# The last block of an attention and two-MLP kernel: six stores on one queue, or three on two

## The chip, the cores and the metric

The kernel runs on 1 core of one Trainium2 chip. The metric is the device time in microseconds of one execution; lower is better. Before the change it is 937.37 us (median of 3 runs, 936.97 to 937.43).

A core has TensorE (PE, matmul; PEld is its weight load), VectorE (DVE), ScalarE (ACT), GpSimd (POOL) and SyncE (SP), which here only issues transfers (DMAs). Transfers are carried by 16 DMA engines.

## The reference

Windowed attention with a bias per head, then two MLPs over 2304 tokens (4 sequences of 576), model width 512, inner width 2048. Scaled input data left out:

```python
def reference(**kwargs):
    ...
    attn_out = _attn_ref(**attn_kwargs)          # softmax(q k^T / 8 - slope*distance, window 128) v
    B, H, S, D = attn_out.shape                  # 4, 8, 576, 64
    x = np.ascontiguousarray(attn_out.transpose(0, 2, 1, 3)).reshape(B * S, H * D)
    x = _moe_ref(x=x, **moe_kwargs)              # g = s*relu(x w_in)^2 + b;  g w_out
    return _moe2_ref(x=x, **moe2_kwargs)         # relu(x w_in)^2 w_out
```

The output `out` has 2304 rows of 512 float32 (2 KB each). Row `b*576 + s` is token `s` of sequence `b`.

## The kernel before

Attention and the first MLP come first; the change does not touch them. Their result stands in device memory in 9 blocks of 256 tokens: two blocks of 256 from each of the 4 sequences, and a ninth, `LAST`, made of the last 64 tokens (`TAIL`) of all four sequences.

The second MLP takes the tokens in three rounds (`n` = 0, 1, 2) of 768, and the inner width in 8 steps (`NP`) each. A round ends with six tiles `t` = 0 to 5 of 128 tokens by 512 columns, summed up in PSUM tiles `po[(n, t)]`. `way_out(n, t)` (line 876) takes such a tile out: a copy from PSUM into a buffer `ob`, by ScalarE for even `t` and by VectorE for odd `t`, and a store from there to `out`. The pair `(n, t)` is half `t % 2` of block `i = (6n + t) // 2`. So tiles 4 and 5 of the last round are the two halves of the ninth block: tile 4 holds the last 64 tokens of sequences 0 and 1, tile 5 those of sequences 2 and 3. Their rows lie in `out` in two groups of 64, 576 rows apart. Before, each group is stored by a transfer of its own (the loop over `a`). Tile 5 of the last round is in addition split by columns in two halves `x` of 256 (`cols`), the first copied by VectorE, the second by ScalarE.

`result(name, staging)` (line 537) hands out the buffers: with staging true the three buffers that go by the tag `st`, else the two that go by `raw`. They are used in turn; who gets one waits until the store out of it, from its last use, has landed.

The order on the engines is that of the program text from line 913 on (`HANDOVER`, then the loop over `k`); the last calls are `behind(23, 0..11)` (line 950), which run the second layer's last matmuls and `way_out(2, 0)` to `way_out(2, 5)` between them. Instructions on one engine run in order; SP's stores stand in one queue in the order of the copies. All instructions carry line 29 (the recorder's), so the trace is read by tile names: `po` is the PSUM tile, `ob` the buffer, `out` the output.

Of the kernel before, what the change touches and what calls it, by code (L numbers as in the profile page):

```python
# [15 lines left out]
P = 128  # L16
# [75 lines left out]
def attention_mlp2_kernel(ctx, tc, first0, first1, qkv0, qkv1, qkvt, w_in1, w_out1, s_in, b_in, w_in2, w_out2, out):  # L92
# [13 lines left out]
    S, D = NT // B, DM // H  # L106
# [5 lines left out]
    BLK = 256  # L112
# [3 lines left out]
    TAIL = S - 2 * BLK  # L116
# [420 lines left out]
    def result(nm, staging=False):  # L537
        if "bp" in pools:
            return pools["bp"].tile([P, DM], F32, tag="st" if staging else "raw", name=nm, bufs=3 if staging else 2)
        return ap.tile([P, DM], F32, tag="pr", name=nm, bufs=NPR)  # L540
# [29 lines left out]
    LAST = len(blocks) - 1  # L570
# [120 lines left out]
    for i, n in ((6, NCC), (8, 2)):  # L691
        for o in range(n):
            x, y = (2 * o, 2 * o + 1) if i == 6 else (o, o + 2)
# [33 lines left out]
    raws, yf, pairs, po = {}, {}, {}, {}  # L727
# [146 lines left out]
                          stop=(k % NP == NP - 1 and j >= 6 and i == 2), skip_group_check=True)  # L874

    def way_out(n, t):
        ob, i, half = result(f"ob{n}{t}", t % 2 > 0), (6 * n + t) // 2, t % 2
        cols = [slice(0, DM)] if n < 2 or t < 5 else [slice(0, BLK), slice(BLK, DM)]
        for x, c in enumerate(cols):
            (act_copy, vector.tensor_copy)[(t + x) % 2](ob[:, c], po[(n, t)][:, c])  # L880
            for a in range(1 if i < LAST else P // TAIL):
                rows = (i // 2) * S + (i % 2) * BLK + half * P if i < LAST else (half * (P // TAIL) + a) * S + 2 * BLK
                size = P if i < LAST else TAIL
                sync.dma_start(out[rows:rows + size, c], ob[a * size:(a + 1) * size, c])

    for k in range(3 * NP):
        for r in range(4):
# [14 lines left out]
    for n in range(3):  # L902
        for q in range(4):
            table[f"Y{n}.{q}"] = lambda n=n, q=q: load_input(n, q)
            for z in range(2):
                table[f"Z{n}.{q}{z}"] = lambda n=n, q=q, z=z: scale_input(n, q, z)
            table[f"T{n}.{q + 1}"] = lambda n=n, i=q + 1: difference(n, i)
        for m in PRODUCTS:
            table[f"V{n}.{m}"] = lambda n=n, m=m: halve_input(n, m)
        for t in range(6):  # L910
            table[f"O{n}.{t}"] = lambda n=n, t=t: way_out(n, t)
# [15 lines left out]
    for k in range(NP, 3 * NP):  # L927
        n, y = divmod(k, NP)
# [66 lines left out]
```

## Time and profile before

| | before |
|---|---|
| median of 3 runs | 937.37 us (936.97 to 937.43) |
| the profiled execution | 937.67 us |
| its span, first to last instruction | 935.9 us |
| TensorE busy | 904.2 us (97%) |
| VectorE, ScalarE busy | 551.7 us (59%), 504.7 us (54%) |
| mean granted TensorE clock | 0.995 of full speed |

The profile is of one execution. Times within it count from the start of its span. The profiled execution's own time has 1.77 us that lie outside the span. Engines are busy with computing instructions; the issue of a transfer is shown on the queue of the engine that issues it (SPq), with the time that the issue takes, and the time to landing is counted from the start of the issue. The share of the DMA engines is the mean of 16. In a strip of 40 digits each digit is the busy share of a slice in tenths (9 is 90% or more).

### The profile page before, as it was taken

How to read it: one execution, taken by the hardware profiler on the slowest of the kernel's cores; microseconds unless marked ns; L12 is line 12 of the kernel's file. 1: busy time of each engine (PE TensorE's matmuls, PEld its weight loads, DVE VectorE, ACT ScalarE, POOL GpSimd, SP SyncE). 2: the span in 40 equal slices, each digit the busy share in tenths (PEclk: the TensorE clock that was granted, in tenths of full speed). 3: DMA queues.
4: the chain of work that ended last, by engine and by line, in shares of the span. 5: the costliest groups of instructions: out<-in, count | busy, mean ns of one | idle time of the engine just before them, and what ended most of it. 6: DMA issues, size and time to landing. Idle time of an engine off the chain costs nothing.

```text
span 935.9 us, 14604 instructions
## 1 busy us (share of the span) xinstructions
PE 904.2 (97%) x5304; PEld 776.0 (83%) x5304; DVE 551.7 (59%) x1345; ACT 504.7 (54%) x1139; POOL 102.3 (11%) x164
## 2 busy tenths in 40 slices
PE   5899999999999999999999999999999999999997
PEld 3789998877787777777898998887889898989896
DVE  7998775455445545545366988787853436443432
ACT  7988776344344444544366877775653335333332
POOL 4343220000000000000022213222000000000000
PEclk9999999999999999999999999999999999999999
DMA  8633523111012101220125655859996666766312
GB/s 314 209 126 118 180 77 106 46 46 40 23 29 90 46 24 45 79 58 23 65 70 205 230 208 191 306 185 354 338 406 209 182 190 180 237 199 194 101 46 68
DMA packets 70216, 136.75 MB, mean 146 GB/s; under 512 B 8576, under 2 KB 36480, under 8 KB 70144
## 3 DMA queue, kind: packets, MB, share of 16 engines
q1 hardware_dynamic: 70144, 135.82, 43.7%
q8 instruction: 42, 0.69, 0.3%
q14 instruction: 30, 0.25, 0.1%
HBM read 103.29 MB, written 32.51 MB: 145 GB/s over the span
## 4 chain that ended last, share of the span: by engine, by line
PE 81%; DVE 7%; ACT 5%; DMA 4%; issue 2%; SPq 0%; POOL 0%; DVEq 0%; ACTq 0%
PE ha L29 20%; PE oa L29 20%; PE po L29 17%; PE px L29 8%; PE py L29 6%; PE s L29 6%; DMA st<-w_in 2%; PE u L29 2%; DVE st L29 1%; DMA rwil<-first 1%; PE s_t L29 1%; DVE tr L29 1%; ACT st L29 1%; DVE m2wih L29 1%; PE u_t L29 1%
## 5 line engine op out<-in xcount | busy, mean ns | idle before, releaser
L29 POOL TENSOR_TENSOR st<-st 128x256 int32<-128x256 int32 x128 | 94.1, 762 | 269.7 <-DVE st L29 254.3
L29 DVE SCALAR_TENSOR_TENSOR r_all<-ha,r_all 128x256 f32<-128x256 f32 (+1 forms) x96 | 52.8, 554 | 99.4 <-ACT r_all L29 99.4
L29 ACT ACTIVATE r_all<-ha 128x256 f32<-128x256 f32 (+1 forms) x96 | 46.5, 488 | 98.8 <-PE ha L29 94.5
L29 ACT ACTIVATE st<-st 128x512 int32<-128x512 uint32 (+3 forms) x100 | 79.9, 817 | 10.6 <-DMA st<-w_in 5.5
L29 PE MATMUL oa<-ga,woh 128*128 128x256 f32 x384 | 72.5, 288 | 0.1
L29 DVE TENSOR_TENSOR tr<-tr 128x384 f32<-128x384 f32 x96 | 55.1, 575 | 22.3 <-ACT tr L29 22.3
L29 ACT ACTIVATE pr<-pr,nd 128x256 f32<-128x256 f32 (+1 forms) x102 | 48.0, 474 | 29.7 <-DVE nd L29 27.5
L29 PEld LDWEIGHTS oa<-ga,woh 128*128 128x128 f32 x384 | 60.1, 191 | 4.6 <-issue 3.5
L29 ACT ACTIVATE tr<-tr 128x384 f32<-128x384 f32 x72 | 37.7, 524 | 40.7 <-DVE tr L29 40.6
L29 PE MATMUL oa<-ga,wol 128*128 128x256 f32 x192 | 54.3, 283 | 0.0
L29 DVE SCALAR_TENSOR_TENSOR st<-st 128x512 int32<-128x512 int32 (+1 forms) x50 | 41.5, 841 | 10.6 <-ACT st L29 10.0
L29 DVE TENSOR_TENSOR tr<-py,tm 128x384 f32<-128x384 f32 x24 | 13.3, 555 | 44.7 <-PE py L29 43.3
L29 DVE TENSOR_TENSOR m2woh<-tr,m2woh 128x384 fp32r<-128x384 f32 x48 | 27.4, 571 | 20.4 <-ACT m2woh L29 18.6
L29 PE MATMUL po<-m2wih,m2woh 128*128 128x512 f32 x144 | 36.6, 395 | 1.3 <-ACT ob L29 0.9
L29 PE MATMUL po<-m2wih,m2wil 128*128 128x512 f32 x144 | 37.7, 392 | 0.0
L29 ACT ACTIVATE m2woh<-tr 128x384 fp32r<-128x384 f32 x48 | 25.2, 525 | 23.2 <-DVE tr L29 22.8
L29 PE MATMUL po<-m2wih,m2wol 128*128 128x512 f32 x144 | 37.6, 392 | 0.0
L29 PE MATMUL ha<-x0h,wih 128*128 128x256 f32 x128 | 37.3, 292 | 0.0
L29 PE MATMUL ha<-x0h,wil 128*128 128x256 f32 x128 | 36.4, 284 | 0.6 <-DVE wil L29 0.6
L29 PEld LDWEIGHTS oa<-ga,wol 128*128 128x128 f32 x192 | 36.7, 191 | 0.0
L29 PE MATMUL ha<-x0l,wih 128*128 128x256 f32 x128 | 36.2, 283 | 0.0
L29 DVE TENSOR_TENSOR tr<-py,r_all 128x384 f32<-128x384 f32 x24 | 13.3, 556 | 38.5 <-ACT r_all L29 38.4
(606 smaller groups left out, 2436.8 us busy)
## 6 DMA issues: line engine op xcount, KB each, us to landing
m2wih<-wd SPq DMA_DIRECT2D x32, 512.0 KB, 4.5
m2woh<-wd SPq DMA_DIRECT2D x22, 512.0 KB, 4.5
st<-w_out SPq DMA_DIRECT2D x20, 512.0 KB, 4.4
st<-w_in SPq DMA_DIRECT2D x8, 1024.0 KB, 6.4
st<-w_in SPq DMA_DIRECT2D x16, 512.0 KB, 4.7
wd<-m2wih SPq DMA_DIRECT2D x16, 512.0 KB, 6.8
m2wil<-wd SPq DMA_DIRECT2D x16, 512.0 KB, 4.6
st<-w_out SPq DMA_DIRECT2D x6, 1024.0 KB, 7.5
```

The costliest lines, as they stand in the source:

```text
L29: ins = op(*args, **kw)
```

## The change

`way_out` asks `result` for a buffer for each half `x` instead of one for each tile, so the second half of the last tile gets one of its own, from the tag that `(t + x) % 2` says (`raw` for tile 5, `x` = 1). The two groups of 64 rows of the last block leave in one transfer, whose place in `out` has the two sequences as its first dimension. The transfer of the last half tile is issued by ScalarE.

```diff
     def way_out(n, t):
-        ob, i, half = result(f"ob{n}{t}", t % 2 > 0), (6 * n + t) // 2, t % 2
+        i, half = (6 * n + t) // 2, t % 2
         cols = [slice(0, DM)] if n < 2 or t < 5 else [slice(0, BLK), slice(BLK, DM)]
         for x, c in enumerate(cols):
-            (act_copy, vector.tensor_copy)[(t + x) % 2](ob[:, c], po[(n, t)][:, c])
-            for a in range(1 if i < LAST else P // TAIL):
-                rows = (i // 2) * S + (i % 2) * BLK + half * P if i < LAST else (half * (P // TAIL) + a) * S + 2 * BLK
-                size = P if i < LAST else TAIL
-                sync.dma_start(out[rows:rows + size, c], ob[a * size:(a + 1) * size, c])
+            ob = result(f"ob{n}{t}{x}", (t + x) % 2 > 0)[:, c]
+            (act_copy, vector.tensor_copy)[(t + x) % 2](ob, po[(n, t)][:, c])
+            if i < LAST:
+                rows = (i // 2) * S + (i % 2) * BLK + half * P
+                sync.dma_start(out[rows:rows + P, c], ob)
+            else:
+                b0 = half * (P // TAIL)
+                (scalar if x else sync).dma_start(out.rearrange("(b s) n -> b s n", s=S)[b0:b0 + P // TAIL, 2 * BLK:, c], ob)
```

The end of SP's queue, before (-) and after (+). The last numbers in a row are the shape on the side of `out`; `DMAHW` are semaphores that landings count up, used in turn, and the others belong to engines.

```order
 L29 DMA out<-ob_8537 128x512 [waits DMAHW0_49,Activation_49]
 L29 DMA out<-ob_8543 128x512 [waits DMAHW1_49,DVE_49]
-L29 DMA out<-ob_8549 64x512 [waits DMAHW2_49,Activation_49]
-L29 DMA out<-ob_8549 64x512 [waits DMAHW3_49]
-L29 DMA out<-ob_8556 64x256 [waits DMAHW4_49,DVE_49]
-L29 DMA out<-ob_8556 64x256 [waits DMAHW5_49]
-L29 DMA out<-ob_8556 64x256 [waits DMAHW6_49,Activation_49]
-L29 DMA out<-ob_8556 64x256 [waits DMAHW7_49]
-L991 UNCONDITIONAL_BRANCH
+L29 DMA out<-ob_8549 2x64x512 [waits DMAHW2_49,Activation_49]
+L29 DMA out<-ob_8555 2x64x256 [waits DMAHW3_49,DVE_49]
```

Tiles 2 and 3 of the last round (8537, 8543) keep their transfers. Tile 4 (8549) goes from two transfers to one, tile 5 (8556) from four to one here, whose shape begins with a 2.

The end of ScalarE's program, before and after: its copies of tiles 2, 4 and of the second half of 5.

```order
 L29 ACTIVATE ob_8537<-po_7799 128x512 [waits DMAHW2_49,PE_49]
 L29 ACTIVATE ob_8549<-po_7819 128x512 [waits DMAHW6_49,PE_49,Activation_49]
-L29 ACTIVATE ob_8556<-po_7823 128x256 [waits DMAHW3_49,DVE_49]
-L991 UNCONDITIONAL_BRANCH
+L29 ACTIVATE ob_8558<-po_7823 128x256 [waits DMAHW0_49,DVE_49,Activation_49]
+L29 DMA out<-ob_8558 2x64x256 [waits DMAHW4_49,Activation_49]
+L994 UNCONDITIONAL_BRANCH
```

The copy of the last half has a buffer of its own (8558) and waits for `DMAHW0`, the semaphore on which the store of tile 2 lands, in place of `DMAHW3`; the transfer out of it stands behind it on ScalarE. On TensorE, VectorE and GpSimd the order of the instructions is the same.

## Rows read from the trace of the kernel before

**Rows 1.** Chain of waits, the last 11 us: start us, us, what.

```profile
924.84 5.00 PE po L29 x22
...
929.87 0.44 DVE ob L29
...
930.32 0.38 ACT ob L29
```

**Rows 2.** The page's first line.

```profile
span 935.9 us, 14604 instructions
```

**Rows 3.** Time line of ScalarE: start us, us, instruction, [idle before it, releaser].

```profile
929.23 0.60 ACT L29 ACTIVATE ob<-po 128x512 f32<-128x512 f32 x1 [0.81 <-PE po L29]
930.32 0.38 ACT L29 ACTIVATE ob<-po 128x256 f32<-128x256 f32 x1 [0.50 <-DVE ob L29]
```

**Rows 4.** Time line of SP's queue, one issue each: start us, us.

```profile
928.60 0.33 SPq L29 DMA_DIRECT2D out<-ob  x1
...
929.86 0.55 SPq L29 DMA_DIRECT2D out<-ob  x1
930.46 0.59 SPq L29 DMA_DIRECT2D out<-ob  x1
...
932.42 0.55 SPq L29 DMA_DIRECT2D out<-ob  x1
933.02 0.59 SPq L29 DMA_DIRECT2D out<-ob  x1
```

**Rows 5.** Single issues (0.74, 927.09, 928.60, 929.86, 933.02 us): KB, us to landing.

```profile
rwih<-first SPq DMA_DIRECT2D x1, 384.0 KB, 3.1
...
out<-ob SPq DMA_DIRECT2D x1, 256.0 KB, 2.0
...
out<-ob SPq DMA_DIRECT2D x1, 256.0 KB, 2.5
...
out<-ob SPq DMA_DIRECT2D x1, 128.0 KB, 2.4
...
out<-ob SPq DMA_DIRECT2D x1, 64.0 KB, 2.0
```

**Rows 6.** DMA view, 926 to 936 us: packets (counts by size add up), and issues.

```profile
DMA packets 1057, 1.58 MB, mean 158 GB/s; under 512 B 160, under 2 KB 416, under 8 KB 1056
...
out<-ob SPq DMA_DIRECT2D x4, 256.0 KB, 2.3
out<-ob SPq DMA_DIRECT2D x2, 128.0 KB, 2.4
out<-ob SPq DMA_DIRECT2D x4, 64.0 KB, 2.0
```

**Rows 7.** DMA view, 929.4 to 930.4 us: packets; queue's packets, MB, share.

```profile
DMA packets 206, 0.38 MB, mean 377 GB/s; under 512 B 25, under 2 KB 25, under 8 KB 205
...
q1 hardware_dynamic: 205, 0.37, 95.9%
```

**Rows 8.** DMA view, 281.2 to 284.8 us, stores of 1 KB rows.

```profile
DMA packets 1025, 0.94 MB, mean 260 GB/s; under 512 B 112, under 2 KB 1025, under 8 KB 1025
...
q1 hardware_dynamic: 1025, 0.94, 74.2%
```

**Rows 9.** DMA view, 931.2 to 932.2 us.

```profile
DMA packets 126, 0.22 MB, mean 221 GB/s; under 512 B 18, under 2 KB 18, under 8 KB 126
...
q1 hardware_dynamic: 126, 0.22, 91.1%
```

**Rows 10.** DMA view, 932.9 to 934.8 us, with its strip of 40 slices.

```profile
DMA  0246895932000003496985300000246895922000
...
DMA packets 240, 0.20 MB, mean 104 GB/s; under 512 B 48, under 2 KB 240, under 8 KB 240
...
q1 hardware_dynamic: 240, 0.20, 40.5%
```

**Rows 11.** DMA view, strip of 933.2 to 933.8 us.

```profile
DMA  5599541506002000000000000000184515699458
```

## The prediction

> **What bounds the kernel now.** I read the chain of waits first. TensorE's last matmuls run to 929.84 us, then VectorE copies one half of the last tile and ScalarE the other, until 930.70 [rows 1]. Yet the span is 935.9 us [rows 2]: 5.2 us in which no engine computes. The time line of SP's queue fills it: ten transfers leave one by one, and from 929.86 us the six of the last block stand 0.6 us apart, the last at 933.02 [rows 4]. The list of transfers says that one lands 2.0 us after its issue [rows 5], so at 935.0. From there to the end of the span are 0.9 us. So the end is the issue of SP, the landing of the last transfer, and 0.9 us. The change moves nothing ahead of TensorE's last matmul; only the two tiles of the last block, 4 and 5 of the last round, matter.
>
> **What the change removes.** Six transfers on SP become two there and one on ScalarE, for the second half of tile 5. SP's last issue thus moves from 933.02 to the place of today's second, 930.46 [rows 4]: 2.56 us of issue gone, if a new transfer takes about 0.55 us as those of 64 rows do (the ones of 128 rows take 0.33; the new one bears 2x64 rows on one side and 128 on the other, so the ends are 0.33 and, unknown, somewhat over 0.59; as the next issue must wait for VectorE's copy until 930.31 anyhow [rows 1], this decides at most 0.3 us).
>
> **What it adds on ScalarE.** In the order, ScalarE's last copy waited for VectorE's (the two wrote one tile). Its half now has a buffer of its own, but the wait for VectorE stays (I take it that it is for the PSUM tile that both read), and one more comes: the new buffer is one of the two that `result` hands out under the tag raw, and it held tile 2 of this round. So the copy waits until the store of tile 2 is home: issued 928.60 [rows 4], landing 2.5 us later [rows 5], 931.1 us. ScalarE therefore starts its copy at about 931.2 and not at 930.32 [rows 3], takes 0.38 us [rows 3], and issues at about 931.7. Nothing is queued behind it but that issue. The wait alone eats 0.9 us of the gain. With the data spread as today this would land 2.0 to 2.4 us later (64 and 128 KB, [rows 5]), at 933.7 to 934.1, 0.9 to 1.3 us before today's 935.0.
>
> **How the data is spread.** Here I expect the decision. The DMA view of the last 10 us counts 1057 packets, of which 160 are under 512 B, 256 more under 2 KB and 640 of 2 KB [rows 6]. The 640 and 256 are just the rows of the ten transfers (4 x 128 + 2 x 64 of 2 KB, 4 x 64 of 1 KB), so a row is a packet; the 160 are 16 for each transfer, one closing packet from each of 16 engines. So a transfer of 128 rows and one of 64 are both dealt out in 16 equal shares of whole rows. The issue time agrees that SP works on the count of rows and not on bytes: 64 rows of 2 KB and 64 rows of 1 KB cost the same 0.55 to 0.59 us, 128 rows of 2 KB cost 0.33 [rows 4]. Every transfer here had 128 or 64 as the first count on both its sides. The new three have 128 in the buffer but 2 in `out`, since the halves of the block lie a whole sequence apart (the order prints 2x64x512 and 2x64x256). Equal shares along the first count on both sides can then only be two, one sequence each, unless the hardware regroups 2x64 as 128, and the two halves of `out` cannot be written as one step. No row shows a transfer with a first count of 2. The ends are 16 engines and 2; rows of that kind lie nearer to 16, but none has a count that 16 does not divide, so I go by what all have in common, shares along the first count, and take 2.
>
> The Trainium skill, "DMA: Bandwidth & Descriptors", section "Why a DMA increments its semaphore by 16 and not by 1", says it as a rule: the largest number of engines up to 16 that divides the slowest dimension of both access patterns, the lowest-numbered ones being used. It speaks against this change: by it 128 and 2 give 2 engines, the same two for all three transfers; the 16 closing packets of each transfer [rows 6] agree with it for 128 and 64. By the rule the sum is the one that follows; with 16 engines it would be the first rival's.
>
> The price then, on two engines. A packet of 2 KB takes 85 ns when the buffers' 128 rows are stored: 95.9% of 16 engines in 1.0 us are 15.3 us, over 205 - 25 = 180 packets [rows 7]. One of 1 KB takes 47 ns: 74.2% of 16 x 3.6 us are 42.7 us, over 1025 - 112 = 913 [rows 8]. Each engine gets 64 rows of tile 4 (64 x 85 ns = 5.4 us) and 64 + 64 half rows of tile 5 (128 x 47 ns = 6.0 us), 11.4 us in all. ScalarE's queue adds an issuer; I take it that it adds no engine, so its half shares the two and is hidden nowhere. The first packet flows 1.2 us after an issue: that of 932.42 begins at 933.62 (slot 28 of 40 in the strip of [rows 11]), so from 929.86 the data begins at 931.1. Until about then the 16 engines have the older tiles. From 931.1 + 11.4 = 942.5, with 0.3 us from the last packet (934.7, the end of the strip in [rows 10]) to the landing (935.0), and 0.9 us to the end: span 943.7 against 935.9, +7.8 us. The profiled execution took 937.67 us, 1.77 outside its span; the median of the runs is 937.37, 0.30 less. So 937.4 + 7.8 = 945.2 us, 0.8% slower.
>
> Ends of this. Upwards: the last tiles' own packets take longer, 135 ns for 2 KB (91.1% of 16 us over 108, [rows 9]) and 64 ns for 1 KB (40.5% of 30.4 us over 192, [rows 10]), in the transfers of 64 rows; I take the quicker prices because those are of transfers with 128 rows in the buffer, as the new ones are, but at these it is 8.6 + 8.2 = 16.8 us, 950.6. Downwards: 85 and 47 ns leave 38 ns per KB and 9 fixed; if two queues on one engine hide the fixed part, 256 x 38 ns = 9.7 us, 943.5. If ScalarE's half were put on two other engines, 5.4 + 3.0 = 8.4 us, 942.2.
>
> **Rivals.** (1) Not slower: the hardware regroups and keeps 16 engines. Then the last landing is ScalarE's at 933.7 to 934.1, the span ends at 934.6 to 935.0, and the time is 936.1 to 936.5 us, about 936.3: 0.1% faster, which no measurement of this kernel tells from no change (about 0.2%, 1.9 us, is what it can tell). For it: every transfer that the trace shows runs on 16. Against: all of those have one count on both sides. Chance 0.16.
> (2) Faster by over 1.9 us: the last landing would have to come by 933.1. ScalarE's half alone can't, at 931.1 + 0.1 + 0.38 + 0.1 + 2.0 = 933.7, unless tile 2 also lands half a microsecond early. Chance 0.02.
> (3) The first transfer on ScalarE's queue pays for a queue that was never used, with 16 engines in use. SP's first in the kernel needed 3.1 us for 384 KB against 2.0 to 2.5 for 256 KB here [rows 5]; that is under 1.1 us of price, and slower by 1.9 us it gets only from 3 us up. It would give some 937 to 939.5. Chance 0.02.
>
> **How the numbers follow.** Two engines 0.80 (shares along the first count explain every transfer of [rows 6]; regrouping is something that no row asks for, though none excludes it), at 945.2 with its own range 942 to 950.6; rival 1 0.16, rival 2 0.02, rival 3 0.02, of which half would count as slower. Slower by over 0.2%: 0.81. Within: 0.17. Faster: 0.02. The range that holds 8 in 10 is that of the two-engine case with a little below it, 941.5 to 950.6; 936.3 is left out knowingly.
>
> **What would show it.** In the profile after, TensorE's last matmul should still end at 929.8 and ScalarE's copy should start at about 931.2, waiting for a transfer out of ob. SP's issues should end near 931.1. If I am right, the DMA view from 931 to 942 shows 2 of 16 engines busy, a share near 0.12 and some 45 GB/s, and 4 x 16 + 3 x 2 = 70 small packets where 160 were. Tile 4's transfer should land some 7 us or more after its issue (today 2.4), the ones of tile 5 near 942.7. I am wrong if the small packets are 112 and the transfers land in under 3 us; then the span ends before 935.2. A size is wrong if the engines are two but the packets take not 85 and 47 ns.

## The result

| | before | after |
|---|---|---|
| median, beside each other | 937.18 us (4 runs, 936.97 to 937.43) | 946.94 us (4 runs, 944.87 to 947.33) |
| ratio to before | | 1.0093, 95% interval 1.0080 to 1.0106 |
| the profiled execution, its span | 937.67 us, 935.9 us | 944.87 us, 943.1 us |
| last matmul's end | 929.8 us | 928.2 us |
| from there to the end of the span | 6.1 us | 14.9 us |

The change makes the kernel 0.9% slower. Two things differ between the two profiled executions. One is luck: the last matmul ends 1.6 us earlier, though nothing ahead of it was moved, and the profiled execution of the changed kernel is the fastest of its four. The other is the stretch behind it, 8.8 us longer. It is the same to a few hundredths of a microsecond in two profiles of the changed kernel (below), while the part ahead of it varies by some microseconds between executions. So the experiments are read by this stretch first, and by the times second.

Time line of ScalarE and of SP's queue after the change, the end; each row is start us, us, instruction, with [idle before it, releaser]. The first row is TensorE's last.

```profile
926.03 2.20 PE L29 MATMUL po<-m2wih,m2wol 128*128 128x512 f32 x9
...
928.26 0.64 SPq L29 DMA_DIRECT2D out<-ob  x1
...
929.01 0.54 SPq L29 DMA_DIRECT2D out<-ob  x1
...
929.58 0.38 ACT L29 ACTIVATE ob<-po 128x256 f32<-128x256 f32 x1 [1.34 <-DMA out<-ob]
929.99 1.15 ACTq L29 DMA_DIRECT2D out<-ob  x1
```

SP is done with its issues 1.3 us after the last matmul (3.8 before, [rows 4]). The wait of ScalarE's last copy that ends last is now, as its releaser says, the one for a transfer out of `ob`; before, it was the one for VectorE [rows 3]. All is issued by 931.1, and the span ends at 943.1. In between SP waits, by the list of its waits from 926 us on (us in total, times, longest; L994 is the end of the program):

```profile
SPq L994 <- DMA out<-ob: 12.4, 1, 12.4
```

From the end of its last issue (929.55) this is until 942.0, when the last transfer has landed.

DMA view of the changed kernel, 928 to 943 us, then 931 to 941: packets (counts by size add up), then each queue's packets, MB and share of 16 engines; q1 is SP's queue, q10 ScalarE's.

```profile
DMA packets 656, 1.00 MB, mean 67 GB/s; under 512 B 38, under 2 KB 294, under 8 KB 656
...
DMA  1011111111111111111111111111111111111111
...
DMA packets 335, 0.45 MB, mean 45 GB/s; under 512 B 4, under 2 KB 230, under 8 KB 335
...
q1 hardware_dynamic: 205, 0.32, 9.2%
q10 hardware_dynamic: 130, 0.13, 3.7%
```

These answer to [rows 6]. The strip of ones is the share of two engines of 16 (12.5%; the two queues have 9.2% + 3.7% = 12.9%), at 45 GB/s, for ten microseconds. A mean share alone could also be 16 engines that are each busy for an eighth of the time; the closing packets decide: the 38 small ones are 16 each for the stores of tiles 2 and 3, and 2 each for the three merged ones.

### The profile page after: what moved, and what is told of

Its sections match the earlier page's. It is cut to its first block, busy times and chain, and to the rows that moved or that the text cites. A ratio compares the mean times of both kernels' runs of the same rounds, so it can differ in the third digit from the quotient of the medians.

```text
span 943.1 us, 14601 instructions
## 1 busy us (share of the span) xinstructions
PE 906.5 (96%) x5304; PEld 779.2 (83%) x5304; DVE 551.6 (58%) x1345; ACT 504.8 (54%) x1139; POOL 102.3 (11%) x164
## 4 chain that ended last, share of the span: by engine, by line
PE 76%; DVE 9%; ACT 7%; DMA 5%; issue 2%; SPq 0%; ACTq 0%; DVEq 0%; POOL 0%
PE ha L29 19%; PE oa L29 19%; PE po L29 15%; PE px L29 8%; PE py L29 6%; PE s L29 6%; DMA st<-w_in 2%; ACT st L29 2%; DVE st L29 2%; PE u L29 2%; DMA st<-w_out 1%; PE s_t L29 1%; DVE tr L29 1%; DVE m2wih L29 1%; DVE m2wil L29 1%
## 5 line engine op out<-in xcount | busy, mean ns | idle before, releaser
L29 PE MATMUL po<-m2wil,m2woh 128*128 128x512 f32 x144 | 36.0, 393 | 0.0
```

The costliest lines, as they stand in the source:

```text
L29: ins = op(*args, **kw)
```

## The experiments

In the table "stretch" is the time from the end of the last matmul to the end of the span in the profiled execution. The ratio is to the kernel before, run beside it.

| run | what is in it | median us | ratio, 95% interval | stretch us |
|---|---|---|---|---|
| before | 2 x 64 rows apart, SP, one buffer | 937.18 | | 6.1 |
| after | merged, ScalarE, own buffer | 946.94 | 1.0093 (1.0080 to 1.0106) | 14.9 |
| after_again | the same | 948.32 | 1.0109 (1.0094 to 1.0124) | 14.9 |
| x1_two_each | apart, ScalarE, own buffer | 938.07 | 1.0004 (0.9994 to 1.0014) | 5.4 |
| x2_merge_only | merged, SP, one buffer | 946.88 | 1.0094 (1.0077 to 1.0111) | 14.7 |
| x4_all_on_sp | merged, SP, own buffer | 946.66 | 1.0093 (1.0078 to 1.0109) | 14.8 |
| x3_tile4_merged | tile 4 alone merged | 941.22 | 1.0029 (1.0019 to 1.0039) | 9.6 |
| x5_127_rows | tile 3 as 127 + 1 rows | 947.37 | 1.0092 (1.0078 to 1.0105) | 14.5 |
| x6_staging_buffer | x1 with a free buffer | 937.66 | 0.9988 (0.9979 to 0.9997) | 4.9 |
| x7_tail_first | last block first | 937.67 | 0.9987 (0.9978 to 0.9996) | 5.4 |
| x8_tail_first_free | the same, free buffers | 937.07 | 0.9990 (0.9981 to 0.9999) | 5.3 |

Theory: the hardware deals a transfer out along its first count, so with 2 in `out` against 128 in the buffer two engines carry it. Rivals: the new wait of ScalarE and its queue cost the time; or a destination with a gap is slow on any number of engines.

**Split the merged transfers again, keep the rest (x1_two_each).**

```diff
-                (scalar if x else sync).dma_start(out.rearrange("(b s) n -> b s n", s=S)[b0:b0 + P // TAIL, 2 * BLK:, c], ob)
+                for a in range(P // TAIL):
+                    rows = (b0 + a) * S + 2 * BLK
+                    (scalar if x else sync).dma_start(out[rows:rows + TAIL, c], ob[a * TAIL:(a + 1) * TAIL])
```

> The changed kernel, but each of its three merged transfers is split again into two of 64 rows; the own buffer, the wait for tile 2's store and ScalarE's queue stay. Theory (two engines carry a transfer whose first count is 2): 16 engines carry everything again, 70 small packets become 160 in the tail, every store lands within 3 us of its issue, and the time falls to 936.3 us (935.5 to 937.4; ScalarE's issue took 1.15 us in the changed kernel, and there are two now). Rival (the wait for tile 2's store and the second queue cost the time): still 944 us or more.

All of the loss is gone (1.0004). In its DMA view from 932 us (its last matmul ends at 932.6) every transfer lands in 2.5 us or less, ScalarE's too, and ScalarE's two transfers bring q10 160 packets: 128 half rows and 2 x 16 small ones.

```profile
q10 hardware_dynamic: 160, 0.13, 8.5%
...
out<-ob SPq DMA_DIRECT2D x2, 64.0 KB, 2.1
out<-ob ACTq DMA_DIRECT2D x2, 64.0 KB, 2.0
```

So wait and queue are not the cause. The stretch is 0.7 us shorter than before, but the medians do not show it: the expected time, 936.3 us, was missed by 1.8. The part ahead of the last matmul hides a gain of this size; in this execution it ended 2.8 us later than in before's.

**Merge alone (x2_merge_only), and the change without ScalarE's queue (x4_all_on_sp).** The first adds to the kernel before:

```diff
+            if i == LAST:
+                b0 = half * (P // TAIL)
+                sync.dma_start(out.rearrange("(b s) n -> b s n", s=S)[b0:b0 + P // TAIL, 2 * BLK:, c], ob[:, c])
+                continue
```

the second changes `(scalar if x else sync)` of the changed kernel to `sync`.

> The kernel before, only with the last block's stores merged to one transfer per piece; one buffer for tile 5, all issued by SP. Theory (two engines): as slow as the change, 946 us (944.5 to 947.5), the two engines have the same 11.4 us of rows each. Rival (wait and second queue): four issues fewer on SP and nothing else, 935.5 to 936.5 us.

> The changed kernel with the last half tile's transfer issued by SP and not by ScalarE. Theory (two engines; the issuer adds no engine): 946 us, within 1.5 us of the changed kernel; if the slow first 3 us of packets (about 150 ns each) come from ScalarE's issue beside them, up to 1.2 us less. Rival (second queue): 936 to 938 us.

Both are as slow as the change, with stretches of 14.7 and 14.8 us. Merging alone makes the loss; who issues is of no account, and the 1.2 us that x4 might have saved without ScalarE's issue did not come. In x2's DMA view, 932 to 944 us, all runs on one queue at two engines' share:

```profile
DMA packets 387, 0.52 MB, mean 43 GB/s; under 512 B 7, under 2 KB 263, under 8 KB 387
...
q1 hardware_dynamic: 387, 0.52, 13.0%
```

**The changed kernel again (after_again).**

> The changed kernel once more, beside the others on one chip, for its spread (its four times went from 944.87 to 947.33 us) and a second profile. Theory: 944.5 to 947.5 us; in the profile the time from the last matmul to the end is again near 14.8 us, and what differs between executions lies ahead of it.

The median, 948.32 us, lies 0.8 us above what was expected; the stretch was as expected. Its rows: last matmul, and the page's first line.

```profile
928.91 2.20 PE L29 MATMUL po<-m2wih,m2wol 128*128 128x512 f32 x9
...
span 946.0 us, 14601 instructions
```

931.1 to 946.0 are 14.9 us, after a last matmul 2.9 us later than in the first profile. In these two profiles the spread of the times lies ahead of the last matmul.

**Half the dose (x3_tile4_merged).** As x2, with `if i == LAST and t == 4:`.

> The kernel before, only with tile 4's two transfers merged to one of 2x64 rows of 2 KB; tile 5 stays with its four. Theory (two engines): 5.4 us of rows on two engines from 931.1 us, and the four small transfers' shares on those two engines behind them; last landing 937.5 to 938.6, so 939.9 to 941.0 us, about a third of the change's loss. Rival (merging itself costs nothing): one issue less on SP, 936.8 us. Rival (any first count of 2 costs a fixed price for each transfer, not one by bytes): also a third, so this run tells the first rival alone.

941.22 us, the stretch 3.5 us longer than before's, 40% of the change's 8.8. The tile has half of the bytes. The time is just above the expected 939.9 to 941.0 us, with the kernel before beside it at 938.39. That the four small transfers suffer too shows in the DMA view from 932.5 to 938 us (last matmul 930.5): the last two land after 6.2 us, where before they took 2.0 [rows 5]. The strip ends with two engines' share, which says that each waits for its shares on the two engines that tile 4 fills.

```profile
DMA  1012411431434579997532114234311111111111
...
out<-ob SPq DMA_DIRECT2D x2, 64.0 KB, 6.2
```

The second rival, a fixed price for each transfer, this run could not tell from the theory. The views of the changed kernel can: the bytes themselves flow at two engines' share until 0.3 us before the last landing (the last packet ends at 941.7 us).

**No gap, no pair, but a bad count (x5_127_rows).** Tile 3, a plain block of 128 rows, in the kernel before:

```diff
+            if n == 2 and t == 3:
+                rows = (i // 2) * S + (i % 2) * BLK + half * P
+                for r in (slice(0, P - 1), slice(P - 1, P)):
+                    sync.dma_start(out[rows + r.start:rows + r.stop, c], ob[r, c])
+                continue
```

> The kernel before, only with the store of tile 3 (128 rows of 2 KB, one plain block in the output) split into 127 rows and 1 row. No first count of 2, no gap in the output. Theory (the number of engines is the largest up to 16 that divides the first count): 127 is prime, one engine carries 254 KB, 127 x 85 ns = 10.8 us from 930.4; the last landing comes at 943 or so, 945 to 947 us. Rival (the gap of a sequence between the two halves, or three-dimensional addresses, make the merged transfer slow): one issue more, 937.4 to 938.5 us.

947.37 us, so a plain block is as slow when its count is 127, a prime. This is 0.4 us above the expected range, with the kernel before beside it at 938.39 us, 1.2 above its 937.18 beside the change. The window view of 932.0 to 935.8 us, the time when the 127 rows are alone (its last three numbers are TensorE's granted clock, the DMA share and GB/s), then SP's issue of the single row behind them, and the packets of the DMA view from 926 to 945.5 us:

```profile
932.00:935.80 3.80, 0.00 (x0) 0.00 (x0) 0.00 (x0) 0.00 (x0) 0.00 (x0) 0.73 0.06 19
...
930.86 4.10 SPq L29 DMA_DIRECT2D out<-ob  x1
...
DMA packets 1043, 1.58 MB, mean 81 GB/s; under 512 B 146, under 2 KB 402, under 8 KB 1042
```

A DMA share of 0.06 is one engine of 16, at 19 GB/s, and the 146 small packets are 16 for each of nine transfers, one for the 127 rows and one for the single row. The gap is not needed for the loss: nothing here has one. The rule of the Trainium skill ("DMA: Bandwidth & Descriptors", section "Why a DMA increments its semaphore by 16 and not by 1"), the largest number up to 16 that divides both counts, thus gives 2 for 2 and 128, 1 for 127 and 16 for 64 and 128, and the traces agree in each case.

**The wait for tile 2's store (x6_staging_buffer).** As x1, and:

```diff
-            ob = result(f"ob{n}{t}{x}", (t + x) % 2 > 0)[:, c]
+            ob = result(f"ob{n}{t}{x}", (t + x) % 2 > 0 or x > 0)[:, c]
```

> As the one with two transfers of 64 rows each, but the last half tile's buffer comes from the three under the tag st, whose last store landed at 930.0, so ScalarE waits only for VectorE. Theory: ScalarE copies at 930.3 and not at 931.2, the last landing at about 933.9, 936.1 us (935.3 to 936.8), about 0.5 to 0.9 us less than the one with the wait. Rival (the wait is hidden behind SP's other transfers): no difference to that one beyond 0.3 us.

ScalarE's last copy in x1, and in x6:

```profile
933.97 0.38 ACT L29 ACTIVATE ob<-po 128x256 f32<-128x256 f32 x1 [1.38 <-DMA out<-ob]
```

```profile
931.45 0.38 ACT L29 ACTIVATE ob<-po 128x256 f32<-128x256 f32 x1 [0.49 <-DVE ob L29]
```

From its last matmul (932.6 and 931.0) that is 1.4 and 0.5 us: the wait is 0.9 us, and the stretch falls by 0.5 (5.4 to 4.9). The rest is hidden behind SP's own transfers: in x1 the last to land is ScalarE's (937.05 us), in x6 SP's (935.02). The median is 937.66 us against 938.39 of the kernel before beside it (0.08% less); the ratio on record is 0.12% below 1, its interval just clear of it. The expected 936.1 us was too low by 1.6, of which 1.2 are before's own (938.39 here, 937.18 above).

**The last block first (x7_tail_first, x8_tail_first_free).** The order of the last calls becomes 0 to 5, 10, 11, 6, 7, 8, 9, tile 3 is the one in two halves, and the last half leaves on ScalarE. In x8 tiles 2 and 3 take buffers of a tag that is free, and ScalarE issues tile 4's two transfers.

```diff
-    behind(3 * NP - 1, *range(12))
+    behind(3 * NP - 1, *range(6), 10, 11, 6, 7, 8, 9)
```

> The last block's two tiles (4 and 5) finish first in the last round, each stored by two transfers of 64 rows, and tile 3 comes last, split by columns into two transfers of 128 rows, the second issued by ScalarE from a buffer of the tag st. Theory: at the end only one short issue stands on each queue; the last landing at 933.0 to 933.6, 935.2 to 935.8 us, 0.15 to 0.2% under the kernel before. Rival (ScalarE's slow issue, or waits for buffers, eat it): 936.5 us or more.

> As the one in which the last block's tiles finish first; in addition tiles 2 and 3 take buffers of a tag that is free by then (yf), so that no copy waits for a store, and the two transfers of tile 4 are issued by ScalarE, so that SP is not late. Theory (what stood in the way there was ScalarE's copy of tile 2, which waited 0.9 us for tile 4's store, and SP's six issues of 0.4 to 0.6 us): the last copy ends 0.9 us after the last matmul, the last landing comes at 3.2 us, the end at 4.0 to 4.2 us after it (6.07 before, 5.43 there); 935.2 to 936.5 us, ratio near 0.998. Rival (two queues at once are slower to land): 4.9 us or more after the last matmul, no better than the one with the staging buffer.

x7's ratio is 0.13% below 1, but its time, 937.67 us, lies above the expected 935.2 to 935.8, and its stretch is 5.4 us where 4.1 to 4.7 had been expected (a landing at 933.0 to 933.6, with the last matmul at 929.8 and 0.9 us behind the landing). ScalarE's copies show a wait that took the place of the old one; both go when the buffers are free, in x8 (the last three rows):

```profile
930.58 0.60 ACT L29 ACTIVATE ob<-po 128x512 f32<-128x512 f32 x1 [1.73 <-DMA out<-ob]
932.13 0.38 ACT L29 ACTIVATE ob<-po 128x256 f32<-128x256 f32 x1 [0.96 <-DMA out<-ob]
```

```profile
929.44 0.60 ACT L29 ACTIVATE ob<-po 128x512 f32<-128x512 f32 x1 [0.19 <-PE po L29]
930.58 0.38 ACT L29 ACTIVATE ob<-po 128x256 f32<-128x256 f32 x1 [0.54 <-DVE ob L29]
930.99 0.36 ACTq L29 DMA_DIRECT2D out<-ob  x1
```

Yet x8's stretch is 5.3 us and not 4.0 to 4.2, its time 937.07 us and not 935.2 to 936.5: my theory fell. ScalarE's copies and issue are where they were expected (the issue at 930.99, 0.9 us after the last matmul at 930.1). But SP is late all the same: its last issue, of tile 3's first half, begins at 931.46 (first row below), 1.4 us after the last matmul, and why was not settled. And the transfers take longer to land, 3.0 us for the 128 KB of either. So the last landing, SP's, comes 4.4 us after the last matmul and not 3.2. The DMA view of x8 from 929 to 934.5 us bears on the landings: the 16 engines' mean share is 8 or 9 tenths from the 14th slice to the 34th, 930.8 to 933.7 us. The last row is of that stretch alone.

```profile
931.46 0.44 SPq L29 DMA_DIRECT2D out<-ob  x1
...
DMA  9699989962697899899989999989999998541000
...
q1 hardware_dynamic: 736, 1.18, 60.4%
q10 hardware_dynamic: 258, 0.30, 20.4%
...
out<-ob ACTq DMA_DIRECT2D x1, 128.0 KB, 3.0
...
DMA packets 682, 1.03 MB, mean 355 GB/s; under 512 B 79, under 2 KB 285, under 8 KB 681
```

The engines are nearly full there, at 355 GB/s, where one queue alone brought them to 377 [rows 7]. So two queues at once look hardly slower than one, and most of the longer landing looks like bytes that wait for an engine; no run tests it. x6, x7 and x8 cannot be told apart by their ratios; x6 has the shortest stretch and the fewest edits, and is the version I would keep. All three ratios are 0.10 to 0.13% below 1 (the medians 0.08 to 0.09%), with intervals that end at 0.9996 to 0.9999.

## Why the prediction was right

- **What bounds the end**: right. Issue, landing, and a rest; TensorE's part was not moved by the change, only by chance (1.6 us earlier in this profile, later in others).
- **SP's issues**: a merged transfer took 0.64 and 0.54 us to issue, near the 0.55 that I took; its cost was no longer of account. That SP works on the count of rows, as I read [rows 4], does not follow from them: 128 rows took less there than 64.
- **ScalarE's new wait**: expected 1.4 us after the last matmul, measured 1.35 (929.58 against 928.23). Its price once the engines are 16: 0.5 us of the end, by x1 and x6, not the 0.9 that I named, as SP's transfers cover the rest.
- **Two engines**: right, by the share, the rate, and the closing packets; split off as the sole cause by x1 and x2, and as a rule of counts by x5.
- **ScalarE's queue adds no engine**: right, by the share of both queues together (12.9%) and by x4. The possibility of two other engines (942.2 us) falls.
- **The price on two engines**: the mis-sized term. I had the last landing 13.0 us behind the last matmul (942.8 - 929.84); it came 13.8 behind (942.0 - 928.2). The prices of 85 and 47 ns hold from 933 us on, but in the first three microseconds far fewer packets flow. DMA view of the changed kernel, 930 to 933, 933 to 936 and 936 to 942 us:

```profile
DMA packets 42, 0.09 MB, mean 29 GB/s; under 512 B 0, under 2 KB 0, under 8 KB 42
...
q1 hardware_dynamic: 42, 0.09, 12.6%
...
q1 hardware_dynamic: 66, 0.14, 11.6%
q10 hardware_dynamic: 18, 0.02, 1.7%
...
q10 hardware_dynamic: 112, 0.11, 5.3%
```

The first has 12.6% of 48 us over 42 packets of 2 KB, 144 ns each on the mean; the second 11.6% of 48 us over 66, 84 ns; the third 5.3% of 96 us over 112 half rows, 45 ns. At 84 ns the two engines would have taken 71 packets in the first three microseconds and not 42: 29 x 84 ns / 2 = 1.2 us lost. That the mean is near the upper price which I had as an end of the range (135 ns) is chance: it is no price of a packet. Most packets take 84 ns here too, as from 931.56 to 931.79 us, where five take 11.4% of 3.68 us (the second row). Between such groups the two engines halt: in the strip from 931.2 to 933 us the high digits are packets that last 0.2 to 0.4 us (a packet counts in the slice in which it begins), with empty slices behind them:

```profile
DMA  0000000112020600002112090000001112040200
...
q1 hardware_dynamic: 5, 0.01, 11.4%
```

The half rows in turn came cheaper than I had them: from 937 to 941 us each of the two engines carries half of 188, one in 42.6 ns and not in 47 (neighbouring packets overlap by a few ns, so shares above come out over 12.5%). Over 128 of them that is 0.6 us won back; with the 1.2 us lost it makes most of the 0.8.

```profile
DMA packets 190, 0.19 MB, mean 48 GB/s; under 512 B 2, under 2 KB 190, under 8 KB 190
```

Why the start has these halts was not settled. They are not chance: the second profile of the changed kernel has 42 packets and 12.6% over the same stretch (932.88 to 935.88 us). They are not ScalarE's issue: it is over at 931.1, and x4, with all on SP, has them too, here from 932.5 to 935.5 us, 1.8 us behind its last matmul as above (there SP's own third issue runs beside them).

```profile
q1 hardware_dynamic: 45, 0.09, 12.6%
```

- **The rest behind the landing**: 0.9 us expected, 1.1 found (942.0 to 943.1).
- **The median**, 946.94 us, lies 1.7 above the forecast: 1.0 us by these two terms (a stretch of 14.9 us for 13.9); the rest I put down to the varying part ahead, which no run shows by itself.

The rivals: 16 engines by regrouping did not happen. A first-use price of ScalarE's queue is not seen: in x1 its two transfers landed in 2.0 us (median), like SP's of that size before.

## What to carry to other kernels

Before two transfers are merged into one, look at the first count on both sides of the merged one: it decides how many of the 16 DMA engines carry it. With 64 and 128 it was all 16 here; a count of 2 left two engines and cost 3.5 us at the end for one tile of 256 KB (x3), a count of 127 left one and cost 8.4 us (x5). Two transfers with 64 rows each, at 0.6 us of issue, are far cheaper than one that has a pair in front. A buffer "of its own" that comes from a pool in rotation brings a wait for the store that last used it, which the releaser of the copy shows.

## What had not been expected of the hardware

An issue lasted far longer than its usual 0.55 us where the engines that it uses had some 128 rows ahead of it; that these rows are the cause is inferred. SP's third merged transfer, behind two of 64 rows for each engine, took 3.52 us to issue in x2 and 3.11 in x4; the single row of x5, behind 127 rows on one engine, took 4.10. The second merged one, with 64 rows ahead, took 0.54. In the changed kernel the third stands alone on ScalarE's queue and took 1.15. In x2 and x4 the rows (SP's queue):

```profile
931.99 3.52 SPq L29 DMA_DIRECT2D out<-ob  x1
```

```profile
932.61 3.11 SPq L29 DMA_DIRECT2D out<-ob  x1
```

In x2 and x4 it cost nothing that shows (stretches of 14.7 and 14.8 us for 14.9), nothing standing behind it; in x5 it held up the six issues behind it until 935.06 us. And a second queue did not get its turn at once: ScalarE's transfer was issued at 929.99 us, yet q10 has no packet from 930 to 933 us and 18 from 933 to 936, where SP's has 66; the cause is open.
